# Batch 0 of a linear-attention kernel: the first q rows by sixteen small activations, dense work begun on one head pair, the other q rows in pairs

## Chip, cores and metric

The kernel runs on one core of a Trainium2 chip. The metric is the time of one launch in microseconds of device time, lower is better. Five engines work beside one another, each on its own list of instructions in order: TensorE (PE), VectorE (DVE), ScalarE (ACT), GpSimd (POOL) and SyncE (SP). Transfers are asked for by SP ("SPq") and by POOL, and are carried out by 16 DMA engines.

## The reference

q, k and v are float32 of shape (8, 8, 576, 64): batch, heads, rows, head size. The two weights are 512 x 2048 and 2048 x 512.

```
q_s = softmax of q over the head size
k_s = softmax of k over the 576 rows
kv  = einsum('bhsd,bhse->bhde', k_s, v)
att = einsum('bhsd,bhde->bhse', q_s, kv)
x   = att, heads joined: 4608 x 512
h   = x @ w_in
out = maximum(0.01 * h, h) @ w_out
```

## The kernel before

One partition holds 9 successive rows of two heads at a time (R = 9 "q rows" per partition, 64 partitions per head; `HL` = 4 head groups), so a q or k tile of one batch is 128 x 4 x 9 x 64. The output is made in nine tiles of 512 tokens (t = 0 to 8). A tile has a first dense layer (`layer1`, 16 column blocks j of w_in; then `leaky` on ACT) and a second (`layer2`, 16 blocks j of w_out). Tile 0 needs 512 of the 576 tokens of batch 0, so nothing dense can run before batch 0's attention; the attention of each later batch is woven into the dense work of earlier tiles. The scheduling is manual: the order of the Python calls is the order on each engine. The function `at(t, u, ...)` hangs calls on place u of tile t: in tile 0, places 0 to 31 follow block j of the first layer (first 256 tokens, then the other 256), and 32 to 47 follow the blocks of the second layer.

Batch 0 goes so (lines of the kernel before):

- L90 to L97: SP asks for q rows 0 to 3 (`RA`), k in two halves, v in two halves, then q rows 4 to 8 (`RB`).
- `q_max`, `q_sub` (POOL), `q_exp` (ACT), `q_sum`, `q_norm` (L221 to L253) are q's softmax: greatest value of each row, subtraction, exponential, sum with reciprocal, product.
- `k_tree` (L151 to L160): four DVE operations that take the maximum over the 9 rows of a partition, for one half (two head groups). `k_max_pe` (L301) turns it with a transpose on PE, `k_all_dve` and `k_all_pe` (L311, L315) take the maximum over partitions and spread it, `k_sub_ps` (L325) subtracts it, `k_exp` (L200) makes the exponential.
- `v_cast` (L207): v to bfloat16. `kv_pair` (L332): k'v for one pair of head groups. `kd_pair` (L346): divides by k's sum and keeps the blocks on the diagonal. `q_transpose`, `q_keep` (L360, L376): q turned on PE and copied out of PSUM. `attend` (L385): q times kv, copied to xT, the input of the dense layer.
- `wake(n)` (L295): n matmuls on zeros whose results are not used.
- POOL's list after setting constants: `q_sub` of rows RA; a copy of one element into `gate` (L483), which waits until k's second half has landed; `load_w_in(0)` (four transfers, the first half of w_in's columns, L133); the two `v_cast`; `load_w_in(1)`; `q_sub` of RB; a second `gate` copy (L525), which waits for k of batch 1; four transfers of w_out (L140). What stands below it on POOL's list follows later: `k_sub` of batch 1 and so on.
- SP's list goes on with `hold_sync(0)` (L521), a small transfer that reads the end of w_in's columns and so waits for the first transfer of `load_w_in(1)`; then k, q, v of batch 1; then `hold_sync(1)`, which waits for a transfer of w_out; then batch 2.
- L532 to L548, hooks of tile 0: rows RB are turned at place 11 and attended at 13; batch 1's k maxima, subtractions and q maxima are called at place 15; batch 1's k'v (`kv(1)`, L261) is at place 38.

PSUM has a ring of six banks (`psB_pool`) for all of these results.

Of the kernel before, what the change touches and what calls it, by code (L numbers as in the profile page):

```python
# [8 lines left out]
FP32 = mybir.dt.float32  # L9
# [11 lines left out]
R = 9  # L21
HL = 4
# [3 lines left out]
def kernel(  # L26
# [112 lines left out]
    def load_w_out(fq):
        nc.gpsimd.dma_start(  # L140
            out=w_out_sb[:, 4 * fq : 4 * fq + 4, :], in_=w_out_r[:, 4 * fq : 4 * fq + 4, :]
        )
# [8 lines left out]
    def k_tree(b, hs):  # L151
        n = hs.stop - hs.start
        ks = st[b]["k"][:, hs]
        t4 = mx_pool.tile([P, HL, 4, D], FP32, name="t4")[:, 0:n]
        nc.vector.tensor_tensor(out=t4, in0=ks[:, :, 0:4], in1=ks[:, :, 4:8], op=ALU.max)  # L155
        t2 = t4[:, :, 0:2]
        nc.vector.tensor_tensor(out=t2, in0=t2, in1=t4[:, :, 2:4], op=ALU.max)  # L157
        t1 = t4[:, :, 0]
        nc.vector.tensor_tensor(out=t1, in0=t1, in1=t4[:, :, 1], op=ALU.max)  # L159
        nc.vector.tensor_tensor(out=st[b]["kmax"][:, hs], in0=t1, in1=ks[:, :, 8], op=ALU.max)  # L160
# [60 lines left out]
    def q_max(b, rs):  # L221
        n = rs.stop - rs.start
        st[b]["qmax", rs.start] = m = small_pool.tile([P, HL, n], FP32, name="qmax")
        nc.vector.tensor_reduce(out=m, in_=st[b]["q"][:, :, rs], axis=AX.X, op=ALU.max)  # L224

    def q_sub(eng, b, rs):
        n = rs.stop - rs.start
        qs = st[b]["q"][:, :, rs]
        eng.tensor_tensor(  # L229
            out=qs,  # L230
            in0=qs,
            in1=st[b]["qmax", rs.start].unsqueeze(3).to_broadcast([P, HL, n, D]),
            op=ALU.subtract,
        )
# [60 lines left out]
    def wake(n):  # L295
        for i in range(n):
            nc.tensor.matmul(  # L297
                wake_ps, lhsT=zero[:, 0:P], rhs=zero, start=(i == 0), stop=(i == n - 1)
            )

    def k_max_pe(b, i):  # L301
        ps = psB_pool.tile([P, 2, L], FP32, name="kT", tag=BANK_TAG)
        nc.tensor.matmul(
            ps.rearrange("c h l -> c (h l)"),
            lhsT=st[b]["kmax"][:, 2 * i : 2 * i + 2].rearrange("p h d -> p (h d)"),
            rhs=identf,
            is_transpose=True,
        )
# [37 lines left out]
    def kd_pair(b, gg):  # L346
        for hh in range(2):
            pkv = st[b]["pkv", gg][hh]
            krec = small_pool.tile([P, 1], FP32, name="krec1")
            nc.vector.reciprocal(out=krec, in_=pkv[:, 128:129])  # L350
            nc.vector.scalar_tensor_tensor(
                out=kd2[b % 2][:, 2 * hh + gg],
                in0=pkv[:, 0:P],
                scalar=krec,
                in1=block,
                op0=ALU.mult,
                op1=ALU.mult,
            )

    def q_transpose(b, r0, n):  # L360
# [57 lines left out]
        else:  # L418
            eng.tensor_copy(out=o, in_=ps)

    def layer1(j, ph, c0, n):
        for i, cb in enumerate((0, 2, 1, 3)):
            nc.tensor.matmul(  # L423
                ph,
                lhsT=w_in_sb[:, cb, j * P : (j + 1) * P],
                rhs=xT[:, cb, c0 : c0 + n],
                start=(i == 0),
                stop=(i == NB - 1),
            )

    def leaky(o, ph):
# [91 lines left out]
    st[1]["q"] = load(q, 1, "q_raw", [(ALLH, ALLR)])  # L523
    st[1]["v"] = load(v, 1, "v_raw", [(ALLH, ALLR)])
    nc.gpsimd.tensor_copy(out=gate[:, 0:1], in_=st[1]["k"][:, 0, 0, 0:1])  # L525
# [12 lines left out]
    at(0, 15, lambda: q_max(1, RA), lambda: q_sub(nc.gpsimd, 1, RA))  # L538
# [125 lines left out]
```

## Time and profile before

Three runs took 302.57, 301.48 and 302.45 us, median 302.45. The profile is of one execution more.

| what | value |
|---|---|
| profiled execution: its time, its span | 300.17 us, 298.4 us |
| PE busy | 283.0 us, 95% of the span |
| DVE, ACT, POOL busy | 151.6, 143.0, 89.0 us |
| chain that ended last, by engine | PE 85%, DVE 8%, ACT 2%, DMA 2%, POOL 1%, issue 1% |
| first dense matmul after which PE has no long wait | 24.31 us after the start |
| PE busy in 24:26 of the span | 1.69 us of 2.00 |
| PE busy in 32:36 of the span | 4.00 us of 4.00 |
| q rows 0 to 3: maximum (DVE), subtraction (POOL), exponential (ACT) | 1.22, 1.90, 1.06 us |
| bytes moved by transfers in the first 60 us | 15.47 MB, mean 258 GB/s |

A line of the timeline or of the chain begins with the start and the duration in us, measured from the span's start. In a timeline line the engine, the line of the kernel, the operation, output and input, shapes and the count follow, and in brackets the idle time of the engine before it with what ended it. A line of the table by stage has the stretch, its length, the busy time of PE, of PE's weight loads, of DVE, ACT and POOL (with the number of instructions), TensorE's granted clock as a share of the full one, the DMA engines' busy share and the bytes moved per second.

### The profile page before, as it was taken

Reading aid. Unit: us, or ns where it says so; the run is one execution under the profiler, and the core shown is the slowest. Engines: PE = TensorE matmul, PEld = TensorE weight load, DVE = VectorE, ACT = ScalarE, POOL = GpSimd, SP = SyncE. Lnnn points to the kernel's source line nnn. Section 1 sums busy time; section 2 is a strip of 40 time slices with the busy share of each in tenths; the row PEclk is TensorE's granted clock in tenths of the full one; section 3 lists DMA queues with packets and bytes.
Section 4 is the critical chain, followed back from the end, with each engine's and each line's share of the span. In section 5 each row is a group of like instructions: output and inputs, shape, how many; then the busy total and the mean of one; then the engine's idle time right before and its main releaser. Section 6 shows DMA issues by size and latency. Waiting matters only on the chain.

```text
span 298.4 us, 4180 instructions
## 1 busy us (share of the span) xinstructions
PE 283.0 (95%) x1638; PEld 138.5 (46%) x1638; DVE 151.6 (51%) x234; ACT 143.0 (48%) x233; POOL 89.0 (30%) x60
## 2 busy tenths in 40 slices
PE   6388999999899999999999999999999999999993
PEld 2137855444444454454445444544454444444441
DVE  3996869691975299079548354835440200110020
ACT  1146675669037903971485428542854066016400
POOL 6926081008008604900940193009400000000000
PEclk9579999999999999999999999999999999999999
DMA  7999999396086844765379137923141310130033
GB/s 260 307 227 384 236 201 375 75 296 250 16 170 196 316 79 106 251 262 115 74 253 335 38 70 250 313 63 70 37 79 35 73 35 0 41 85 16 0 73 70
DMA packets 36371, 45.75 MB, mean 153 GB/s; under 512 B 15872, under 2 KB 18944, under 8 KB 36352
## 3 DMA queue, kind: packets, MB, share of 16 engines
q1 hardware_dynamic: 33088, 41.30, 46.7%
q0 software_dynamic: 3264, 4.20, 8.0%
q8 instruction: 13, 0.21, 0.3%
q14 instruction: 6, 0.05, 0.1%
HBM read 36.70 MB, written 9.44 MB: 155 GB/s over the span
## 4 chain that ended last, share of the span: by engine, by line
PE 85%; DVE 8%; ACT 2%; DMA 2%; POOL 1%; issue 1%; SPq 0%; POOLq 0%
PE pout L444 40%; PE ph L423 39%; PE pkv L268 3%; PE po L411 2%; DMA k_raw<-in_k_dram 2%; DVE t L155 1%; POOL k_raw L193 1%; DVE t L157 1%; DVE k_raw L328 1%; ACT vb L211 1%; DVE kmax L160 1%; DVE t L159 1%; ACT xT L397 1%; DVE xT L399 1%; PE psum_qt L364 1%
## 5 line engine op out<-in xcount | busy, mean ns | idle before, releaser
L444 PE MATMUL pout<-w_out_sb,gj 128*128 128x512 bf16 x576 | 130.9, 380 | 0.7 <-DVE out_sb L438 0.7
L423 PE MATMUL ph<-xT,w_in_sb 128*128 128x512 bf16 (+1 forms) x640 | 127.4, 358 | 0.7 <-DVE xT L399 0.6
L432 ACT ACTIVATE gj<-ph 128x512 bf16<-128x512 f32 x144 | 82.6, 603 | 58.8 <-PE ph L423 58.1
L423 PEld LDWEIGHTS <-w_in_sb 128*128 128x128 bf16 x640 | 62.2, 98 | 62.8 <-issue 1.9
L444 PEld LDWEIGHTS <-gj 128*128 128x128 bf16 x576 | 55.8, 98 | 63.0 <-issue 1.0
L438 DVE COPY out_sb<-pout 128x512 f32<-128x512 f32 x36 | 24.5, 687 | 88.9 <-PE pout L444 83.2
L193 POOL TENSOR_TENSOR k_raw<-k_raw,kall 128x2304 f32<-128x2304 f32 (+1 forms) x6 | 29.1, 4844 | 92.1 <-DVE kall L185 76.0
L229 POOL TENSOR_TENSOR q_raw<-q_raw,qmax 128x2304 f32<-128x2304 f32 (+2 forms) x10 | 32.7, 3273 | 29.5 <-DVE qmax L224 24.0
L246 DVE TENSOR_REDUCE qsum<-qe 128x36 f32<-128x2304 bf16 (+2 forms) x10 | 20.7, 2072 | 38.7 <-ACT qe L237 38.6
L417 ACT CAST xT<-po 128x320 bf16<-128x320 f32 (+1 forms) x48 | 16.8, 402 | 39.4 <-PE po L411 39.4
L201 ACT ACTIVATE ke<-k_raw 128x2304 bf16<-128x2304 f32 (+1 forms) x10 | 17.4, 1737 | 24.6 <-POOL k_raw L193 15.6
L224 DVE TENSOR_REDUCE qmax<-q_raw 128x36 f32<-128x2304 f32 (+2 forms) x10 | 20.5, 2061 | 4.8 <-DMA q_raw<-in_q_dram 4.8
L253 DVE TENSOR_TENSOR qe<-qe,qrec 128x2304 bf16<-128x2304 bf16 (+2 forms) x10 | 20.8, 2078 | 0.3
L237 ACT ACTIVATE qe<-q_raw 128x2304 bf16<-128x2304 f32 (+2 forms) x10 | 17.4, 1744 | 6.3 <-POOL q_raw L229 6.3
L213 POOL CAST vb<-v_raw 128x1152 bf16<-128x1152 f32 x14 | 16.0, 1170 | 0.0
L155 DVE TENSOR_TENSOR t<-k_raw 128x1024 f32<-128x1024 f32 (+1 forms) x10 | 11.6, 1165 | 0.5 <-DMA k_raw<-in_k_dram 0.3
L297 PE MATMUL pout<-zero 128*128 128x512 bf16 x24 | 10.0, 595 | 1.3 <-POOL zero L100 1.3
L411 PE MATMUL po<-qX,kd 128*128 128x320 bf16 (+1 forms) x48 | 9.8, 286 | 0.0
L268 PEld LDWEIGHTS <-ke 64*128 64x128 bf16 x252 | 7.2, 93 | 3.3 <-ACT gj L432 1.7
L268 PE MATMUL pkv<-vb,ke 64*128 64x129 bf16 x252 | 8.6, 217 | 0.2 <-ACT vb L211 0.2
L286 DVE TENSOR_TENSOR kd<-pkv,krec 64x128 bf16<-64x128 f32 x28 | 8.1, 288 | 0.7
L411 PEld LDWEIGHTS <-kd 128*128 128x128 bf16 x48 | 4.6, 98 | 5.9 <-DMA qX<-qe 0.5
(50 smaller groups left out, 90.9 us busy)
## 6 DMA issues: line engine op xcount, KB each, us to landing
out_dram<-out_sb SPq DMA_DIRECT2D x72, 128.0 KB, 2.4
q_raw<-in_q_dram SPq DMA_DIRECT2D x7, 1152.0 KB, 8.2
v_raw<-in_v_dram SPq DMA_DIRECT2D x7, 1152.0 KB, 11.4
k_raw<-in_k_dram SPq DMA_DIRECT2D x6, 1152.0 KB, 5.8
k_raw<-in_k_dram SPq DMA_DIRECT2D x4, 576.0 KB, 5.2
w_in_sb<-in_moe_w_in_dram POOLq DMA_DIRECT2D x8, 256.0 KB, 6.0
w_out_sb<-in_moe_w_out_dram POOLq DMA_DIRECT2D x4, 512.0 KB, 13.4
v_raw<-in_v_dram SPq DMA_DIRECT2D x2, 576.0 KB, 7.5
```

Source lines behind the costliest of these rows:

```text
L193: eng.tensor_tensor(out=ks, in0=ks, in1=st[b]["kall"][:, hs].unsqueeze(2).to_broadcast([P, n, R, D]), op=ALU.subtract,)
L201: nc.scalar.activation(out=st[b]["ke"][:, :, hs].rearrange("p r h d -> p h r d"), in_=st[b]["k"][:, hs], func=AF.Exp,)
L224: nc.vector.tensor_reduce(out=m, in_=st[b]["q"][:, :, rs], axis=AX.X, op=ALU.max)
L229: eng.tensor_tensor(out=qs, in0=qs, in1=st[b]["qmax", rs.start].unsqueeze(3).to_broadcast([P, HL, n, D]), op=ALU.subtract,)
L246: nc.vector.reduce_sum(out=qsum, in_=st[b]["qe"][:, rs], axis=AX.X)
L253: nc.vector.tensor_tensor(out=qes, in0=qes, in1=st[b]["qrec", rs.start].unsqueeze(3).to_broadcast([P, n, HL, D]), op=ALU.mult,)
L268: nc.tensor.matmul(pkv[hh][:, gg, 0:129], lhsT=st[b]["ke"][rows, r, 2 * gg : 2 * gg + 2].rearrange("p h d -> p (h d)"), rhs=vb2[b % 2][row ...
L411: nc.tensor.matmul(ps.rearrange("p (r l) -> p r l", l=L), lhsT=kd2[b % 2][:, g], rhs=qX[:, gg, hh, rs])
L423: nc.tensor.matmul(ph, lhsT=w_in_sb[:, cb, j * P : (j + 1) * P], rhs=xT[:, cb, c0 : c0 + n], start=(i == 0), stop=(i == NB - 1),)
L432: nc.scalar.activation(out=o, in_=ph, func=AF.Prelu, alpha=LEAKY_SLOPE)
L438: nc.vector.tensor_copy(out=out_sb, in_=pout)
L444: nc.tensor.matmul(pout, lhsT=g_sb[j // 2][:, j % 2, tsub * P : (tsub + 1) * P], rhs=w_out_sb[:, j, :], start=(j == 0), stop=(j == NF - 1),)
```

## The change

The q rows of batch 0 are cut anew: RA stays rows 0 to 3; RB is cut into R1 (rows 4, 5), R2 (rows 6, 7) and R3 (row 8). In the order of the lists:

- SP asks for rows RA in two transfers of 256 KB (heads 0 and 1, then 2 and 3) where there was one of 512 KB.
- Rows RA: `q_max`, the subtraction on POOL, one exponential of 128 x 1024 and one sum on DVE are replaced by `q_first`: two DVE maxima that write the negated value, and sixteen ACT exponentials of 128 x 64, each with its row's negated maximum as a bias and an added sum output. The reciprocal of the sums stays on DVE (`q_first_rec`).
- On DVE, `k_all_dve(0, 0)` stands after the first operation of the second half's tree; the first half's `k_sub_ps` is cut in two by head group, with an exponential after each. `q_max` of rows RB no longer stands ahead of `kd`.
- `q_keep` of the second half of RA goes from ACT to DVE. One of the four diagonal blocks is made on ACT by two scalings of 64 x 64.
- `wake` goes from 12, 4 and 8 matmuls to 16, 1, 1, 2 and 1.
- The first 256 tokens: six blocks j begin with the contributions of heads' pairs 0 and 2, in three banks, before `attend(0, [1, 3])`, and are finished after it.
- POOL's list is now: gate; `load_w_in(0)`; two `v_cast`; `load_w_in(1)`; `q_sub` of R1; the second gate, which waits for k of batch 1; five transfers of w_out (blocks 0-1, 2-3, 4-7, 8-11, 12-15) where there were four; `q_sub` of R2; `q_sub` of R3; `k_sub` of batch 1 and so on.
- ACT's list in tile 0 is: three `leaky`; exponential of R1; one `leaky`; exponential of R2; three `leaky`; xT of pairs 0 and 2; four `leaky`; exponential of R3; and so on.
- DVE's list after `kd` is: `q_max` R1, `q_max` R2; sum, reciprocal and product of R1, the same of R2; `q_keep` of R1 and of R2; xT of pairs 1 and 3; `q_max` R3; then the k tree of batch 1.
- PE's list: R1 is turned at place 9, R2 at place 12 (between the matmuls of j = 12 and j = 13), both are attended at place 14; R3, which tile 1 needs first, is turned at place 37 and attended at 40. Batch 1's hooks stay where they were.

```diff
+    R1, R2, R3 = slice(4, 6), slice(6, 8), slice(8, R)
-    st[0]["q"] = load(q, 0, "q_raw", [(ALLH, RA)])
+    st[0]["q"] = load(q, 0, "q_raw", [(slice(0, 2), RA), (slice(2, 4), RA)])
...
+    def q_first(b, rs):
+        n = rs.stop - rs.start
+        nmax = small_pool.tile([P, HL, n], FP32, name="nmax")
+        qsum = small_pool.tile([P, n, HL], FP32, name="qsum")
+        for hs in (slice(0, 2), slice(2, 4)):
+            nc.vector.tensor_reduce(
+                out=nmax[:, hs], in_=st[b]["q"][:, hs, rs], axis=AX.X, op=ALU.max, negate=True
+            )
+            for h in range(hs.start, hs.stop):
+                for r in range(n):
+                    nc.scalar.activation(
+                        out=st[b]["qe"][:, rs.start + r, h],
+                        in_=st[b]["q"][:, h, rs.start + r],
+                        func=AF.Exp,
+                        bias=nmax[:, h, r : r + 1],
+                        accum_out=qsum[:, r, h : h + 1],
+                    )
+        st[b]["qsum"] = qsum
...
+        if eng is nc.scalar:
+            for p0 in range(0, P, D):
+                ps = slice(p0, p0 + D)
+                nc.scalar.mul(out=o[ps, ps], in_=pkv[ps, ps], mul=krec[ps])
...
-    wake(12)
+    HA, HB = slice(0, 1), slice(1, 2)
+    wake(16)
     k_begin(0)
     q_begin(0)
-    q_max(0, RA)
-    q_sub(nc.gpsimd, 0, RA)
+    q_first(0, RA)
     nc.gpsimd.tensor_copy(out=gate[:, 0:1], in_=st[0]["k"][:, HL - 1, R - 1, D - 1 : D])
     load_w_in(0)
     k_tree(0, H0)
     k_max_pe(0, 0)
-    wake(4)
-    k_tree(0, H1)
-    k_max_pe(0, 1)
+    wake(1)
+    k_tree(0, H1, slice(0, 1))
     k_all_dve(0, 0)
     k_all_pe(0, 0)
+    k_tree(0, H1, slice(1, 4))
+    k_max_pe(0, 1)
+    wake(1)
+    k_sub_ps(0, 0, HA)
+    k_exp(0, slice(0, 1))
     k_all_dve(0, 1)
     k_all_pe(0, 1)
-    wake(8)
-    q_exp(0, RA)
-    q_sum(0, RA)
-    k_sub_ps(0, 0)
-    k_exp(0, H0)
+    wake(2)
+    k_sub_ps(0, 0, HB)
+    k_exp(0, slice(1, 2))
     k_sub_ps(0, 1)
     k_exp(0, H1)
     v_cast(nc.gpsimd, 0, 0)
     v_cast(nc.gpsimd, 0, 1)
     load_w_in(1)
+    q_first_rec(0, RA)
     q_norm(0, RA)
-    q_max(0, RB)
-    q_sub(nc.gpsimd, 0, RB)
     kv_pair(0, 0)
+    wake(1)
     q_transpose(0, 0, 4)
     kv_pair(0, 1)
+    for hh in range(2):
+        kd_rec(0, 0, hh)
+        kd_one(nc.vector, 0, 0, hh)
     q_keep(nc.scalar, 0, 0, 4, slice(0, 4, 2))
-    kd_pair(0, 0)
-    q_keep(nc.scalar, 0, 0, 4, slice(1, 4, 2))
+    q_keep(nc.vector, 0, 0, 4, slice(1, 4, 2))
+    kd_rec(0, 1, 1)
+    kd_one(nc.scalar, 0, 1, 1)
+    kd_rec(0, 1, 0)
+    kd_one(nc.vector, 0, 1, 0)
     attend(0, [0, 2], 0, 256, nc.scalar)
-    kd_pair(0, 1)
-    attend(0, [1, 3], 0, 256, nc.vector)
-    q_exp(0, RB)
-    q_sum(0, RB)
-    q_norm(0, RB)
+    q_max(0, R1)
+    q_sub(nc.gpsimd, 0, R1)
...
-    for fq in range(4):
-        load_w_out(fq)
+    for j0, j1 in ((0, 2), (2, 4), (4, 8), (8, 12), (12, 16)):
+        load_w_out(slice(j0, j1))
...
-    at(0, 11, lambda: q_transpose(0, 4, 3), lambda: q_transpose(0, 7, 2))
-    at(0, 11, lambda: q_keep(nc.vector, 0, 4, 3), lambda: q_keep(nc.vector, 0, 7, 2))
-    for g in range(NB):
-        at(0, 13, lambda g=g: attend(0, [g], 256, 320, (nc.scalar, nc.vector)[g % 2]))
+    at(0, 5, lambda: q_max(0, R2), lambda: q_sub(nc.gpsimd, 0, R2))
+    at(0, 5, lambda: q_exp(0, R1), lambda: q_sum(0, R1), lambda: q_norm(0, R1))
+    at(0, 7, lambda: q_exp(0, R2), lambda: q_sum(0, R2), lambda: q_norm(0, R2))
+    at(0, 9, lambda: q_transpose(0, 4, 2), lambda: q_keep(nc.vector, 0, 4, 2))
+    at(0, 12, lambda: q_transpose(0, 6, 2), lambda: q_keep(nc.vector, 0, 6, 2))
+    at(0, 14, lambda: attend(0, [0, 2], 256, 256, nc.scalar))
+    at(0, 14, lambda: attend(0, [1, 3], 256, 256, nc.vector))
+    at(0, 15, lambda: q_max(0, R3), lambda: q_sub(nc.gpsimd, 0, R3))
+    at(0, 21, lambda: q_exp(0, R3))
+    at(0, 32, lambda: q_sum(0, R3), lambda: q_norm(0, R3))
+    at(0, 37, lambda: q_transpose(0, 8, 1), lambda: q_keep(nc.scalar, 0, 8, 1))
+    at(0, 40, lambda: attend(0, [0, 1, 2, 3], 512, 64, nc.scalar))
...
+    begun = []
+    for j in range(0, 6, 2):
+        ph = psB_pool.tile([P, 2, 256], FP32, name="ph", tag=BANK_TAG)
+        for i in range(2):
+            layer1(j + i, ph[:, i], 0, 256, slice(0, 2), i == 0)
+        begun.append(ph)
+    attend(0, [1, 3], 0, 256, nc.scalar)
     for half in range(2):
         for j in range(0, NF, 2):
-            ph = psB_pool.tile([P, 2, 256], FP32, name="ph", tag=BANK_TAG)
+            part = slice(2, 4) if begun else slice(0, 4)
+            ph = begun.pop(0) if begun else psB_pool.tile([P, 2, 256], FP32, name="ph", tag=BANK_TAG)
             for i in range(2):
-                layer1(j + i, ph[:, i], 256 * half, 256)
+                layer1(j + i, ph[:, i], 256 * half, 256, part, i == 0, i == 1)
```

More of the change, by code (lines that the diff above doesn't have):

```diff
@@ L137, with load_w_out @@
     w_out_r = moe_w_out.rearrange("(fb f) o -> f fb o", f=P)
[L139 to L142, printed above, removed]
+    def load_w_out(js):
+        nc.gpsimd.dma_start(out=w_out_sb[:, js, :], in_=w_out_r[:, js, :])
     def k_begin(b):
@@ L149, in k_begin, with k_tree @@
         st[b]["kall"] = mx_pool.tile([P, HL, D], FP32, name="kall")
-    def k_tree(b, hs):
+    def k_tree(b, hs, steps=slice(0, 4)):
         n = hs.stop - hs.start
         ks = st[b]["k"][:, hs]
[L154 to L160, printed above, removed]
+        if steps.start == 0:
+            st[b]["t4"] = mx_pool.tile([P, HL, 4, D], FP32, name="t4")[:, 0:n]
+        t4 = st[b]["t4"]
+        t2, t1 = t4[:, :, 0:2], t4[:, :, 0]
+        for o, i0, i1 in (
+            (t4, ks[:, :, 0:4], ks[:, :, 4:8]),
+            (t2, t2, t4[:, :, 2:4]),
+            (t1, t1, t4[:, :, 1]),
+            (st[b]["kmax"][:, hs], t1, ks[:, :, 8]),
+        )[steps]:
+            nc.vector.tensor_tensor(out=o, in0=i0, in1=i1, op=ALU.max)
     def k_allmax(b):
@@ L224, in q_max, with q_first_rec @@
         nc.vector.tensor_reduce(out=m, in_=st[b]["q"][:, :, rs], axis=AX.X, op=ALU.max)
+    def q_first(b, rs):
[16 more added lines that the diff above has]
+        st[b]["qsum"] = qsum
+    def q_first_rec(b, rs):
+        n = rs.stop - rs.start
+        st[b]["qrec", rs.start] = qrec = small_pool.tile([P, n, HL], FP32, name="qrec")
+        nc.vector.reciprocal(out=qrec, in_=st[b]["qsum"])
     def q_sub(eng, b, rs):
@@ L323, in k_all_pe, with k_sub_ps @@
         st[b]["kallp", i] = ps
-    def k_sub_ps(b, i):
-        ks = st[b]["k"][:, 2 * i : 2 * i + 2]
-        a = st[b]["kallp", i].rearrange("p (h d) -> p h d", d=D)
+    def k_sub_ps(b, i, hs=slice(0, 2)):
+        ks = st[b]["k"][:, 2 * i + hs.start : 2 * i + hs.stop]
+        a = st[b]["kallp", i].rearrange("p (h d) -> p h d", d=D)[:, hs]
+        n = hs.stop - hs.start
         nc.vector.tensor_tensor(
-            out=ks, in0=ks, in1=a.unsqueeze(2).to_broadcast([P, 2, R, D]), op=ALU.subtract
+            out=ks, in0=ks, in1=a.unsqueeze(2).to_broadcast([P, n, R, D]), op=ALU.subtract
         )
@@ L344, in kv_pair, with kd_rec, kd_one @@
         st[b]["pkv", gg] = pkv
[L346 to L350, printed above, removed]
-            nc.vector.scalar_tensor_tensor(
[L352 to L357, printed above, removed]
+    def kd_rec(b, gg, hh):
+        st[b]["krec", gg, hh] = krec = small_pool.tile([P, 1], FP32, name="krec1")
+        nc.vector.reciprocal(out=krec, in_=st[b]["pkv", gg][hh][:, 128:129])
+    def kd_one(eng, b, gg, hh):
+        pkv, krec = st[b]["pkv", gg][hh], st[b]["krec", gg, hh]
+        o = kd2[b % 2][:, 2 * hh + gg]
+        if eng is nc.scalar:
+            for p0 in range(0, P, D):
+                ps = slice(p0, p0 + D)
+                nc.scalar.mul(out=o[ps, ps], in_=pkv[ps, ps], mul=krec[ps])
+        else:
+            nc.vector.scalar_tensor_tensor(
+                out=o, in0=pkv[:, 0:P], scalar=krec, in1=block, op0=ALU.mult, op1=ALU.mult
             )
@@ L419, in attend_x, with layer1 @@
             eng.tensor_copy(out=o, in_=ps)
-    def layer1(j, ph, c0, n):
-        for i, cb in enumerate((0, 2, 1, 3)):
+    def layer1(j, ph, c0, n, part=slice(0, 4), first=True, last=True):
+        for i, cb in list(enumerate((0, 2, 1, 3)))[part]:
             nc.tensor.matmul(
@@ L426, in layer1 @@
                 rhs=xT[:, cb, c0 : c0 + n],
-                start=(i == 0),
-                stop=(i == NB - 1),
+                start=(i == 0 and first),
+                stop=(i == NB - 1 and last),
             )
```

## The prediction

> **What bounds the kernel now.** I read the chain that ended last first: it is PE without a gap worth naming from 24.31 us on, save one short wait at 46.2, and a DVE chain ahead of it. So a change to batch 0 counts in two places: when the dense work gets going, and whether it then runs on without waiting. From the chain, the place where RB is turned and the end of batch 1's chain:
>
> ```profile
> 24.31 5.18 PE ph L423 x46
> 29.50 0.56 PE psum_qt L364 x10
> 30.05 0.87 PE ph L423 x8
> ...
> 32.19 0.61 DVE t L155
> ...
> 45.13 1.06 ACT vb L211
> 46.18 0.04 issue
> 46.23 0.69 PE pkv L268 x18
> ```
>
> PE waits a little at 46.23 for ACT's cast, which ends a chain that began on DVE at 32.10 (tree of batch 1). PE alone would have been there at about 45.4, so batch 1's chain, 14.1 us from the tree's start, is ahead of PE by 0.9 us: whoever delays the tree delays the end.
>
> The timeline of DVE shows what the change is after. The same four operations take 1.81 us at 32.10 and 5.0 us at 6.26, where POOL works on SBUF beside them:
>
> ```profile
> 6.26 2.25 DVE L155 TENSOR_TENSOR t<-k_raw 128x512 f32<-128x512 f32 x1 [0.29 <-DMA k_raw<-in_k_dram]
> ...
> 9.32 1.27 DVE L160 TENSOR_TENSOR kmax<-t,k_raw 128x128 f32<-128x128 f32 x1
> ...
> 11.35 1.25 DVE L157 TENSOR_TENSOR t<-t 128x256 f32<-128x256 f32 x1
> ...
> 32.10 0.68 DVE L155 TENSOR_TENSOR t<-k_raw 128x512 f32<-128x512 f32 x1
> 32.82 0.42 DVE L157 TENSOR_TENSOR t<-t 128x256 f32<-128x256 f32 x1
> ```
>
> The timeline of POOL shows the row that decides, to my mind:
>
> ```profile
> 21.43 2.33 POOL L229 TENSOR_TENSOR q_raw<-q_raw,qmax 128x1280 f32<-128x1280 f32 x1 [5.51 <-DVE krec L350]
> 24.03 0.19 POOL L525 COPY gate<-k_raw 128x1 f32<-128x1 f32 x1 [0.27 <-DMA k_raw<-in_k_dram]
> 24.49 3.04 POOL L140 DMA_DIRECT2D w_out_sb<-in_moe_w_out_dram  x4 [0.28 <-issue]
> ```
>
> The second gate waits for batch 1's k, which lands at 24.0, and the w_out issues hold POOL until 27.53. Before the change all of RB's subtraction is over by then; R2's and R3's now stand behind it. What sets 24.0 is in the table by stage: SP asks for that k from 19.29, but bytes move at some 209 GB/s (w_in) until about 21.5 and only then at 410.
>
> ```profile
> 20.00:21.00 1.00, 0.99 (x24) 0.90 (x26) 1.00 (x1) 0.35 (x2) 0.00 (x0) 1.00 1.12 209
> 21.00:22.00 1.00, 0.38 (x11) 0.16 (x5) 0.93 (x5) 0.74 (x2) 0.57 (x1) 1.00 1.10 267
> 22.00:23.00 1.00, 0.64 (x3) 0.19 (x2) 0.93 (x5) 0.35 (x1) 1.00 (x1) 1.00 1.04 410
> ```
>
> The DMA engines' share (second number from the end) is above 1 from 4 us to here, so this k comes when everything asked for before it is through. The change asks for the same bytes in the same order: 24.0 stays, within 0.5 us.
>
> **The front, part by part.** k's first half lands at 6.2, as before; the two half maxima of q (0.67 us each, from 1.22 for 1024 elements) are over before it. The extra issue of q puts k back by 0 to 0.45 us (one SP issue); I take 0, since the engines are filled with q meanwhile. DVE then: tree without POOL's subtraction 1.81, first operation of the next 0.72, kr 0.3, rest of the tree 1.1, one collision with the w_in issues as at 9.32 (0.98; 0 to 2): 11.2. k_sub half, kr, half, whole: 0.67 + 0.3 + 0.67 + 1.3, to 14.1. Reciprocal and q_norm 0.17 + 1.2, to 15.5; two kd 0.92. PE: transposes 0.62 and kv_pair 0.7, to 16.8; q_keep on DVE, two small ACT scalings (0.2 each, as the 0.206 of one element), xT 0.58: 18.2. Twelve matmuls at 0.113 are 1.35, attend 0.3, xT 0.6: 20.5, with twelve matmuls done where before there were two at 24.31. The front gains 24.31 - 20.5 + 10 x 0.113 = 4.9 us. Removed from DVE's path are 1.14 (sum), 1.4 (qmax of RB) and some 3 of collisions.
>
> The sixteen small exponentials have no row. From below: 0.206 us each (the one-element row), 3.3 together; from above two such rows, one of them for the sum, and 0.06 for 64 elements at the 0.9 ns that lie between the ACT rows of 512 and 1024: 0.47, 7.6 together, for the one of 1.06 removed. They start at about 4.3 and are wanted by 13.9, so either end is covered. The cover goes at 0.6 us each on that path.
>
> The Trainium skill, "ScalarE: Activation LUTs", section "What ACT_TABLE_LOAD costs", speaks against this edit: an activation with a pointer bias costs a fixed 280 ns or so beside 0.833 ns per element, and neighbours overlap by about 93 ns. That would be an estimated 0.24 us each, 3.8 us together; no row here shows it, and the end would be the same.
>
> **The wait that replaces it.** PE goes on from 20.5: twelve second halves 1.35, sixteen matmuls 1.8, R1 turned when its q_norm is done (three leaky at 0.6 after 20.95, exponential 0.62, then 1.6 on DVE: 24.9; PE waits 1.25), 0.28, then twelve matmuls up to j = 12 at 26.55. There it needs R2 normalized. R2, from rows: gate at 24.03, issue from 24.49; three transfers of 0.774 and two of half size at 0.39 to 0.774, I take 0.65 (near the 0.617 of a w_in issue): 3.6, to 28.1 (27.6 to 28.4). POOL's subtraction of 512 elements 1.04 (line through 1.896 for 1024 and 2.327 for 1280): 29.15. Exponential 0.62 (same way): 29.8; ACT stands still for it, its leaky queued behind. Sum, reciprocal, product 0.67 + 0.20 + 0.68 and gaps: 31.4. Transposes 0.28: 31.7. So PE stands some 4.9 us, and the front's gain is spent here whatever it was.
>
> After that: j = 13 and 14 0.9, four attends 0.5, xT 0.7, qmax of R3 0.4, to 34.25, where batch 1's tree begins; before it was 32.10: +2.15. POOL's subtraction of R3 (256 elements, 0.6) falls on the tree's first operation, as it did at 6.26: 0 to 0.6, I take 0.3. Batch 1's chain keeps its 14.1 us behind that, its w_out and v transfers being no later: +2.45 (1.9 to 3.1) at 46.23. PE itself would be later by 31.7 + 0.1 for R3's transposes, against 30.34 for j = 13 before: 1.5, less than the chain, so it waits 1 us there. Behind 46.2 PE was full, so the shift stays to the end. R3's own steps (DVE 1 us, ACT 0.8, from the rows by size) lie where DVE had waited 3.2 us at 45.16, and ahead of ACT's q_keep at 49.87; there is nothing to charge.
>
> **The clock.** The granted clock fell at 8.57, 2.6 us after the last wake's end at 5.96, and came back at 18.8, after 4.7 us of nearly unbroken matmuls:
>
> ```profile
> 8.50:8.75 0.25, 0.00 (x0) 0.00 (x0) 0.22 (x2) 0.25 (x1) 0.25 (x2) 0.65 1.03 387
> ...
> 18.75:19.00 0.25, 0.25 (x2) 0.00 (x0) 0.25 (x2) 0.16 (x2) 0.00 (x0) 0.87 1.17 221
> ```
>
> A stand of 4.9 us is longer than 2.6, so the work behind it may begin at half clock. The blocks and attends before xT would then cost 1.4 us more (0.9 + 0.5 again); PE's own 4.7 us at half rate lose 2.35, to 3.85 late, as much as the chain. So 0 to 1.4, and I take 0.7: a few idle microseconds may fall across two of whatever stretches the clock is judged by. A slow clock already in the front (fewer wakes) costs at most the front's 5 us and is covered by the same stand.
>
> The Trainium skill, "TensorE: Matmul & The Clock Gate", Part 1, has the clock fall after an idle window of about 3.4 us that runs free of the kernel, and return after as much sustained work. By that the loss is an estimated 1.7 us of PE, which the chain's lead would partly hide; the sum would stay at its warm or its cold end by where the window falls.
>
> **Sum.** +2.45 + 0.7 = +3.15: 303.3 against the profiled 300.17, and 305.6 against the median of the runs, 302.45, which lies 2.3 above that execution. This is the time I give; the case's own range is +1.9 to +4.5, 304.3 to 307.0.
>
> **Rivals.** (1) Faster: k of batch 1 lands early enough for POOL to get to R2 in time. Then R2 is normalized at 26.3 and PE does not stand; the tree begins at about 29.5 and batch 1's chain ends 2.6 us earlier: 299.8. The tree starts 6.15 after R2's subtraction does, so the break-even is a start at 25.7, a landing at 21.6. For it speaks that 18.62, when SP is let through, is early; against it that w_in fills the engines until 21.5. Chance 0.17. (2) No change: landing near 21.6, or part of the shift made up where ACT and PE interleave at 50 to 58 (the chain there has waits of under 0.1 us, which speaks against it): 302.5. Chance 0.12. (3) The small activations or the front pass the 4.9 us of cover: at 1.1 us each the sums end at 22 where 14 was wanted, 8 late, 3.1 beyond the cover: 302.45 + 3.15 + 3.1, about 309. No row is near that price. Chance 0.04.
>
> **How the numbers follow.** The forecast has 0.67. Half a per cent, 1.5 us, is about what a measurement of this kernel can tell from no change. Slower by more: forecast and rival 3, 0.71; within it 0.12; faster 0.17. For 8 in 10 I leave out rival 1's lower half and rival 3: 300.3 to 307.8.
>
> **What would show it.** Right: R2's subtraction on POOL starts at about 28, directly behind the w_out issues; PE idles 3 to 5 us ahead of R2's transposes near 31.5; batch 1's tree starts at 34 to 35; the first half's tree takes under 2 us at 6.3. Wrong: the second gate before 22, R2's transposes before 28, or matmuls behind the stand that run unbroken with batch 1's tree before 32.

## The result, and the profile after

The changed kernel takes 309.46 us (median of four runs, 309.00 to 310.09) against 302.42 us for the kernel before beside it (four runs, 301.48 to 302.57): a ratio of 1.0241, 95% interval 1.0211 to 1.0270. So it is slower, as forecast, but by 7.0 us where 3.15 were forecast, and 309.46 lies outside the stated range of 300.3 to 307.8. The profiled execution took 310.09 us with a span of 308.2; its mean granted clock was 0.97, before 0.983.

The timeline of the changed kernel, with start and duration in us, shows the place that the prediction turned on:

```profile
10.74 0.30 POOL L514 COPY gate<-k_raw 128x1 f32<-128x1 f32 x1 [6.73 <-DMA k_raw<-in_k_dram]
...
29.69 0.19 POOL L561 COPY gate<-k_raw 128x1 f32<-128x1 f32 x1 [5.26 <-DMA k_raw<-in_k_dram]
...
30.16 3.72 POOL L141 DMA_DIRECT2D w_out_sb<-in_moe_w_out_dram  x5 [0.28 <-issue]
...
33.85 1.09 POOL L257 TENSOR_TENSOR q_raw<-q_raw,qmax 128x512 f32<-128x512 f32 x1
34.98 0.63 ACT L265 ACTIVATE qe<-q_raw 128x512 bf16<-128x512 f32 x1 [4.17 <-POOL q_raw L257]
...
37.44 0.58 PE L395 MATMUL psum_qt<-ident,qe 128*128 128x128 bf16 x4 [3.59 <-DVE qe L281]
...
41.55 0.68 DVE L163 TENSOR_TENSOR t<-k_raw 128x512 f32<-128x512 f32 x1
```

From the second gate downward it is the forecast's story: gate, w_out issues, R2's subtraction behind them, exponential, R2's transposes with PE standing ahead of them, then batch 1's tree. But the gate opens at 29.69, not at 24.03. The first gate is late as well (10.74, before 7.90, where it came straight behind POOL's subtraction of RA). In the changed kernel both wait for a transfer of k. Batch 1's tree is 9.45 us later than before (32.10), its last k'v 9.73 us later (55.96 for 46.23), and the span is 9.8 us longer: nothing is won or lost behind that.

The chain that ended last has transfers in it that were not there before. Its early part (start, duration, engine, what):

```profile
2.26 8.42 DMA k_raw<-in_k_dram
...
15.68 7.47 DMA w_in_sb<-in_moe_w_in_dram
23.83 5.74 DMA k_raw<-in_k_dram
30.16 3.72 POOL w_out_sb L141 x5
```

In the table by stage the last number is GB/s and the one ahead of it the DMA engines' busy share. Two stretches of the kernel before:

```profile
4.00:6.00 2.00, 1.96 (x7) 0.52 (x4) 1.22 (x1) 0.00 (x0) 0.01 (x1) 1.00 1.04 409
...
18.00:20.00 2.00, 1.69 (x21) 0.66 (x19) 2.00 (x3) 1.91 (x2) 0.00 (x0) 0.80 1.12 209
```

The same stretches of the changed kernel:

```profile
4.00:6.00 2.00, 2.00 (x7) 0.60 (x5) 0.98 (x2) 1.57 (x9) 0.01 (x1) 1.00 0.83 206
...
18.00:20.00 2.00, 2.00 (x21) 0.99 (x19) 1.97 (x3) 1.13 (x2) 0.08 (x1) 0.50 1.09 158
36.00:40.00 4.00, 2.56 (x15) 1.93 (x16) 1.98 (x5) 1.18 (x3) 0.00 (x0) 0.66 1.23 218
```

Half the bytes move in 4:6, while k of batch 0 is under way, and a quarter fewer in 18:20, while w_in is; in 18:20 the engines are as busy as before. The trace holds each packet's duration. k's packets (2304 bytes) that start between 3.5 and 6 us, and w_in's (2048 bytes) between 16 and 22 us, in ns:

```
kernel        k packets  median  95%   longest    w_in packets  median  95%  longest
before            361       93     93     101          578         173    173     173
changed           197       93    412    1704          475         173    360     766
```

Most packets are as quick as before, and a few take up to 18 times as long. The last line of the table above (36:40) shows the clock (third number from the end) at 0.66 behind PE's stand.

### The profile page after: what moved, and what is told of

It reads as the page before. It is cut to its first block, busy times and chain, and to the rows that moved or that the text cites. A ratio compares the mean times of both kernels' runs of the same rounds, so it can differ in the third digit from the quotient of the medians.

```text
span 308.2 us, 4204 instructions
## 1 busy us (share of the span) xinstructions
PE 284.0 (92%) x1613; PEld 139.9 (45%) x1639; DVE 150.8 (49%) x241; ACT 148.6 (48%) x270; POOL 88.1 (29%) x62
## 4 chain that ended last, share of the span: by engine, by line
PE 79%; DMA 7%; POOL 4%; DVE 3%; ACT 2%; issue 1%; SPq 1%; POOLq 0%; ACTq 0%
PE pout L475 38%; PE ph L454 36%; DMA k_raw<-in_k_dram 5%; DMA w_in_sb<-in_moe_w_in_dram 2%; PE pkv L296 2%; PE po L442 2%; POOL k_raw L196 1%; POOL w_out_sb L141 1%; DVE t L163 1%; POOL w_in_sb L134 1%; ACT vb L214 1%; POOL vb L216 1%; ACT xT L428 1%; ACT qe L265 1%; PE psum_qt L395 1%
## 5 line engine op out<-in xcount | busy, mean ns | idle before, releaser
L454 PE MATMUL ph<-xT,w_in_sb 128*128 128x512 bf16 (+1 forms) x627 | 129.2, 362 | 3.2 <-ACT xT L428 2.2
L274 DVE TENSOR_REDUCE qsum<-qe 128x36 f32<-128x2304 bf16 (+4 forms) x11 | 19.8, 1800 | 45.8 <-ACT qe L265 45.8
L257 POOL TENSOR_TENSOR q_raw<-q_raw,qmax 128x2304 f32<-128x2304 f32 (+4 forms) x11 | 31.8, 2894 | 34.0 <-DVE qmax L227 34.0
L204 ACT ACTIVATE ke<-k_raw 128x2304 bf16<-128x2304 f32 (+2 forms) x11 | 17.6, 1597 | 24.6 <-POOL k_raw L196 15.6
L281 DVE TENSOR_TENSOR qe<-qe,qrec 128x2304 bf16<-128x2304 bf16 (+4 forms) x12 | 22.2, 1851 | 0.4
L227 DVE TENSOR_REDUCE qmax<-q_raw 128x36 f32<-128x2304 f32 (+4 forms) x11 | 19.5, 1788 | 0.0
L265 ACT ACTIVATE qe<-q_raw 128x2304 bf16<-128x2304 f32 (+4 forms) x11 | 16.8, 1525 | 4.3 <-POOL q_raw L257 4.2
L163 DVE TENSOR_TENSOR t<-k_raw 128x1024 f32<-128x1024 f32 (+1 forms) x10 | 10.1, 1010 | 4.4 <-DMA k_raw<-in_k_dram 4.2
L163 DVE TENSOR_TENSOR t<-t 128x256 f32<-128x256 f32 (+2 forms) x20 | 10.8, 540 | 0.6
L395 PE MATMUL psum_qt<-ident,qe 128*128 128x128 bf16 x36 | 3.5, 228 | 5.8 <-DVE qe L281 5.8
```

Source lines behind the costliest of these rows:

```text
L163: nc.vector.tensor_tensor(out=o, in0=i0, in1=i1, op=ALU.max)
L257: eng.tensor_tensor(out=qs, in0=qs, in1=st[b]["qmax", rs.start].unsqueeze(3).to_broadcast([P, HL, n, D]), op=ALU.subtract,)
L265: nc.scalar.activation(out=st[b]["qe"][:, rs].rearrange("p r h d -> p h r d"), in_=st[b]["q"][:, :, rs], func=AF.Exp,)
L274: nc.vector.reduce_sum(out=qsum, in_=st[b]["qe"][:, rs], axis=AX.X)
L281: nc.vector.tensor_tensor(out=qes, in0=qes, in1=st[b]["qrec", rs.start].unsqueeze(3).to_broadcast([P, n, HL, D]), op=ALU.mult,)
L454: nc.tensor.matmul(ph, lhsT=w_in_sb[:, cb, j * P : (j + 1) * P], rhs=xT[:, cb, c0 : c0 + n], start=(i == 0 and first), stop=(i == NB - 1 a ...
```

## The experiments

The time of the kernel before on the chips of these runs was 300.65 (runs 1 to 4), 301.68 (5 to 8), 301.34 (9 to 11) and 300.76 us (12). "k lands" is the start of the first operation of batch 0's tree, which waits for k.

| kernel | median us | ratio to before, 95% interval | k lands | second gate | tree of batch 1 |
|---|---|---|---|---|---|
| before | | | 6.26 | 24.03 | 32.10 |
| changed | 309.46 | 1.0241 (1.0211 to 1.0270) | 9.19 | 29.69 | 41.55 |
| 1 changed, once more | 308.13 (one run) | | 8.69 | 27.89 | 39.75 |
| 2 R2 ahead of the gate | 303.04 | 1.0066 (1.0034 to 1.0099) | 8.00 | 27.38 | 31.59 |
| 3 one load of q | 303.99 | 1.0106 (1.0086 to 1.0125) | 6.62 | 24.60 | 35.01 |
| 4 old softmax of RA | 308.68 | 1.0239 (1.0192 to 1.0287) | 8.93 | 30.18 | 42.01 |
| 5 before, with the cut | 301.24 | 0.9989 (0.9965 to 1.0013) | 8.39 | 28.65 | 31.02 |
| 6 both of 2 and 3 | 302.18 | 1.0022 (0.9998 to 1.0047) | 6.44 | 24.68 | 32.58 |
| 7 6 with the old softmax of RA | 303.49 | 1.0080 (1.0051 to 1.0109) | 6.50 | 25.68 | 34.61 |
| 8 changed, cut by rows | 308.73 | 1.0225 (1.0172 to 1.0278) | 8.46 | 28.53 | 40.40 |
| 9 6 with v casts on ACT | 299.46 | 0.9932 (0.9910 to 0.9954) | 6.52 | 25.14 | 31.32 |
| 10 9 with earlier exponentials | 298.81 | 0.9911 (0.9882 to 0.9941) | 6.37 | 25.38 | 30.50 |
| 11 before, v casts on ACT | 298.66 | 0.9922 (0.9892 to 0.9952) | 6.37 | 24.82 | 31.40 |
| 12 10 with more dummy matmuls | 298.39 | 0.9912 (0.9890 to 0.9935) | 6.45 | 24.90 | 28.99 |

**1. The changed kernel once more.** Nothing is edited; the question is whether the slow transfers belong to the kernel or to one execution.

> The changed kernel once more, to see whether its slow transfers belong to it. In its first profile batch 0's k landed at 9.2 us (6.2 before the change) and batch 1's k at 29.7 (24.0). If the kernel makes the transfers slow, both come again within 1 us and the time is 309 to 310. If they were chance, they land at about 6.2 and 24 and the time is the 305 to 306 of the prediction's sum.

k lands at 8.69, the gate opens at 27.89, and k's packets in 3.5 to 6 us again include long ones (longest 1442 ns). The delay belongs to the kernel; its size varies by some 2 us (the gate is 1.8 us earlier than in the first profile, and the one time is 308.13, where 309 to 310 was expected).

**2. R2 ahead of the second gate.** The forecast's mechanism is taken away; the cut load stays.

```diff
     q_sub(nc.gpsimd, 0, R1)
+    q_max(0, R2)
+    q_sub(nc.gpsimd, 0, R2)
...
-    at(0, 5, lambda: q_max(0, R2), lambda: q_sub(nc.gpsimd, 0, R2))
```

> R2's maximum and subtraction called before the second gate, all else as changed. Theory of the wait (R2's subtraction stands behind the gate and the w_out issues on POOL): PE no longer stands ahead of R2's transposes, batch 1's tree starts at about 36.4 instead of 41.55, time about 304.4. If only the late landing counts and not what is queued behind it, the time stays at 309.

```profile
20.06 2.04 POOL L257 TENSOR_TENSOR q_raw<-q_raw,qmax 128x512 f32<-128x512 f32 x2 [3.04 <-DVE qmax L227]
...
27.38 0.19 POOL L563 COPY gate<-k_raw 128x1 f32<-128x1 f32 x1 [5.27 <-DMA k_raw<-in_k_dram]
...
28.93 0.38 PE L395 MATMUL psum_qt<-ident,qe 128*128 128x128 bf16 x4
...
31.59 0.68 DVE L163 TENSOR_TENSOR t<-k_raw 128x512 f32<-128x512 f32 x1
```

The timeline shows both subtractions done at 22.1, R2's transposes without a wait, and batch 1's tree half a microsecond earlier than in the kernel before, although the gate still opens 3.4 us late. The ratio falls from 1.0241 to 1.0066. What hangs on the gate, then, is R2, as the prediction had it. The tree is far earlier than the 36.4 that I had expected, and the time 1.4 us below the expected 304.4. But this profile is of the fastest of ten executions (300.70 to 304.96 us), and in it DVE's last tree operation of batch 0 took 0.29 us at 12.31, where the changed kernel's took 2.37 (more in run 9). So not all of the 9.96 us by which the tree is earlier need come from the edit, and the 0.7% that remain can't be read from this profile.

**3. One load of q.** The order behind the gate stays; only the cut is undone.

```diff
-    st[0]["q"] = load(q, 0, "q_raw", [(slice(0, 2), RA), (slice(2, 4), RA)])
+    st[0]["q"] = load(q, 0, "q_raw", [(ALLH, RA)])
```

> The first q rows asked for in one transfer again, all else as changed. Theory that the cut transfer slows the others: batch 0's k lands at about 6.2, batch 1's at about 24, time 305 to 306. Rival, that the small activations or something else slows them: 9.2, 29.7 and 309 as before.

```profile
24.60 0.19 POOL L561 COPY gate<-k_raw 128x1 f32<-128x1 f32 x1 [2.50 <-DMA k_raw<-in_k_dram]
25.06 3.72 POOL L141 DMA_DIRECT2D w_out_sb<-in_moe_w_out_dram  x5 [0.27 <-issue]
...
28.75 1.10 POOL L257 TENSOR_TENSOR q_raw<-q_raw,qmax 128x512 f32<-128x512 f32 x1
...
32.34 0.39 PE L395 MATMUL psum_qt<-ident,qe 128*128 128x128 bf16 x4 [2.05 <-DVE qe L281]
...
35.01 0.68 DVE L163 TENSOR_TENSOR t<-k_raw 128x512 f32<-128x512 f32 x1
```

This is, in its order, the timeline that the prediction described: gate within 0.6 us of 24.0, tree 10.41 us behind it (10.22 in the prediction's sum), tree to last k'v 14.40 (14.1). The time is 3.3 us above the kernel before, 3.15 in the forecast. The transfers are quick again (the longest of w_in's packets in 16 to 22 us takes 173 ns). So what the changed kernel loses beyond the forecast goes with the cut. (I had expected 305 to 306 us, reckoned from a kernel before at 302.45; on this chip it took 300.65.) That the loss agrees so closely is in part luck: PE stood 2.05 us ahead of R2's transposes, not 4.9, and the clock stayed at 1.00 behind it, so the 0.7 us charged for the clock didn't occur; a gate 0.57 us late and 0.19 us more from the gate to the tree took their place.

**4. The old softmax of RA, with the cut.** This asks whether the ACT work of the small exponentials, or their reading of q, disturbs the transfers.

```diff
-    q_first(0, RA)
+    q_max(0, RA)
+    q_sub(nc.gpsimd, 0, RA)
...
+    q_exp(0, RA)
+    q_sum(0, RA)
-    q_first_rec(0, RA)
```

> The first q rows by the old steps (maximum, subtraction on POOL, one exponential, sum on DVE), all else as changed, the two transfers of q too. Theory that the sixteen small activations with sums slow the transfers: batch 0's k lands at 6.2 to 6.7 and batch 1's at about 24, time 305 to 306.5 (POOL's subtraction meets the tree again, which the stand ahead of R2 hides). Rival, that the cut transfer or something else does: 9.2, 29.7, 309 to 310.

The transfers are as slow without the small exponentials: k lands at 8.93, the gate opens at 30.18, the time is that of the changed kernel.

**5. The kernel before with only the cut.**

```diff
-    st[0]["q"] = load(q, 0, "q_raw", [(ALLH, RA)])
+    st[0]["q"] = load(q, 0, "q_raw", [(slice(0, 2), RA), (slice(2, 4), RA)])
```

> The kernel before with nothing but the first q load cut in two by heads. Theory that the cut alone slows the transfers: batch 0's k lands at 8 to 9.2 us instead of 6.2, batch 1's at 27 to 30 instead of 24, and the time is 3 to 5 us over the kernel before. Rival, that the cut only hurts beside the other edits (more wakes, no work of POOL's at the start): 6.2 to 6.7, 24 and no change.

```profile
20.21 2.33 POOL L229 TENSOR_TENSOR q_raw<-q_raw,qmax 128x1280 f32<-128x1280 f32 x1 [2.94 <-DVE krec L350]
...
28.65 0.19 POOL L525 COPY gate<-k_raw 128x1 f32<-128x1 f32 x1 [6.11 <-DMA k_raw<-in_k_dram]
...
31.02 0.68 DVE L155 TENSOR_TENSOR t<-k_raw 128x512 f32<-128x512 f32 x1
```

I had expected a loss of several microseconds, and there is none (0.9989). The transfers are slow here too: k at 8.39, gate 4.6 us late, k packets up to 1542 ns. But in this kernel nothing of batch 0 stands behind the second gate: rows RB are subtracted at 20.21, ahead of it. And k's lateness at the front is paid back, since POOL's subtraction of RA is over (7.63) when k's tree begins, and the tree's first half runs in 1.8 us instead of 4.3. The same cut costs this kernel nothing and the changed one 3.7 us: that loses 7.0 us with the cut and 3.3 without it (run 3). The two kernels differ in more than the place of the subtraction; run 6 compares the two orders in one kernel.

**6. Both repairs.** The edits of 2 and 3 together.

> The change with both repairs: R2's subtraction before the second gate, and q in one load. If the two account for the whole loss and their costs add: the time is that of the kernel before within 1 us (batch 1's tree near 32.1; the front lost 2 to 3 us to the casts on POOL against the sum in the prediction). If the front's gain of 4.9 is there as predicted, 2 to 3 us faster than before. If something else is slower still, 302 or more against 300.65.

1.0022 (0.9998 to 1.0047): no measurable loss is left, and no gain. Cut and order together account for the 2.4%, and the change as a whole wins nothing yet. The tree of batch 1 starts at 32.58, 0.5 us later than before. Runs 2, 3 and 6 with the changed kernel make up all four cases: with R2 behind the gate the cut costs 1.35% (1.0241 against 1.0106), with R2 ahead of it 0.44% (1.0066 against 1.0022, whose intervals overlap).

**7. Run 6 with the old softmax of RA.** The edit of run 4 on run 6, with RA's one exponential called earlier, ahead of the first `k_sub_ps`.

> As the run with both repairs, but the first q rows by the old steps (maximum on DVE, subtraction on POOL, one exponential, sum on DVE). If the sixteen small activations gain what the prediction's front says (1.2 of sum and reciprocal on DVE, and POOL's subtraction off the tree, 1.6): 2 to 3 us slower than with both repairs. If the front is hidden behind R1's and R2's normalization or w_in's landing: the same within 0.5 us.

The tree's first operation takes 2.25 us again under POOL's subtraction, batch 1's tree is 2.0 us later than in run 6, and the time 1.3 us longer. That is what the small exponentials, in place of the old steps, are worth where nothing covers it, less than the 2 to 3 us that I had expected.

**8. The cut made by rows.** Heads stay together; rows 0, 1 and rows 2, 3 are loaded apart.

```diff
-    st[0]["q"] = load(q, 0, "q_raw", [(slice(0, 2), RA), (slice(2, 4), RA)])
+    st[0]["q"] = load(q, 0, "q_raw", [(ALLH, slice(0, 2)), (ALLH, slice(2, 4))])
```

> The changed kernel with the first q load cut by rows (0, 1 and 2, 3; all heads in each) instead of by heads. If any second transfer at the front upsets the others: batch 0's k lands at 8 to 9.5, time 307 to 310. If it is the cut by heads: k lands at 6.5 to 7 (the packets are half as large, some 0.3 us more), batch 1's at 24 to 25, time 304 to 306.

The same as the changed kernel: k at 8.46, gate at 28.53, k packets up to 1694 ns. It isn't this cut by heads, but two loads where there was one. What in the second load does it is not taken apart: in all six profiles with the cut SP also asks for k half a microsecond later (at 1.75, before at 1.25), and no run delays k without the cut.

**9. The v casts on ACT.** In run 6 DVE's last tree operation of batch 0 took 2.39 us instead of 0.29, beside POOL's two v casts; the changed kernel has the same at 13.56:

```profile
11.84 1.69 DVE L163 TENSOR_TENSOR t<-t 128x256 f32<-128x256 f32 x2
13.51 2.27 POOL L216 CAST vb<-v_raw 128x1152 bf16<-128x1152 f32 x2
13.56 2.37 DVE L163 TENSOR_TENSOR kmax<-t,k_raw 128x128 f32<-128x128 f32 x1
```

So the casts go to ACT, which stands idle there.

```diff
+    v_cast(nc.scalar, 0, 0)
     wake(1)
     k_sub_ps(0, 0, HA)
...
     k_exp(0, slice(1, 2))
+    v_cast(nc.scalar, 0, 1)
...
-    v_cast(nc.gpsimd, 0, 0)
-    v_cast(nc.gpsimd, 0, 1)
```

> The changed kernel with one first q load and with R2's maximum and subtraction ahead of the second gate (302.18 us, kernel before 302.4 to 302.5 in all runs so far), and with batch 0's two v casts moved from POOL to ACT, where ACT has waits of 2.81 and 0.86 us. Theory (the front's gain was eaten by VectorE's last tree operation, 10.79 for 2.39 us, held through the two casts): that operation takes 0.29 us, batch 0's chain is about 1.7 us earlier at its k'v, the first dense matmul too, batch 1's tree starts near 30.9 instead of 32.58, and the time is 300 to 301 us, 0.992 to 0.996 of the kernel before. Rival (the dense work's start was not what bounded it, since R1's exponential waits behind three leaky and w_in's and k's transfers don't move): 301.7 to 302.5, tree of batch 1 after 32.

The timeline of this run at the same operations, with POOL's w_in issues beside them:

```profile
8.31 4.93 POOL L134 DMA_DIRECT2D w_in_sb<-in_moe_w_in_dram  x8
...
9.17 0.74 DVE L163 TENSOR_TENSOR t<-t 128x256 f32<-128x256 f32 x2
9.94 0.29 DVE L163 TENSOR_TENSOR kmax<-t,k_raw 128x128 f32<-128x128 f32 x1
```

The three operations take 1.03 us instead of 4.06, and 0.9932 of the kernel before is reached. The tree of batch 1 starts at 31.32, a little behind the 30.9 expected. (The kernel before had been at 300.65 and 301.68 us in the runs up to here, not at 302.4 to 302.5.)

**10. Earlier exponentials of R1 and R2.** In run 6 DVE waits 5.01 us for R1's exponential, which stands behind three `leaky` on ACT.

```diff
-    at(0, 5, lambda: q_exp(0, R1), lambda: q_sum(0, R1), lambda: q_norm(0, R1))
-    at(0, 7, lambda: q_exp(0, R2), lambda: q_sum(0, R2), lambda: q_norm(0, R2))
+    at(0, 1, lambda: q_exp(0, R1), lambda: q_sum(0, R1), lambda: q_norm(0, R1))
+    at(0, 3, lambda: q_exp(0, R2), lambda: q_sum(0, R2), lambda: q_norm(0, R2))
```

> The same, with the exponentials, sums and products of R1 and R2 hooked behind blocks 1 and 3 instead of 5 and 7, so that R1's exponential stands behind one leaky and R2's behind two. Theory: VectorE's wait of 5.01 us for R1's exponential shrinks, PE's wait of 1.47 us at R1's transposes goes, batch 1's tree starts near 29.7, and the time is 298.5 to 300 us, 0.986 to 0.993 of the kernel before, the fastest of all. Rival: ACT then delays leaky and with it the banks of PE, what is won at the tree is lost there: the same as the kernel without the earlier hooks within 0.5 us.

PE's wait at R1's transposes goes from 1.47 to 0.49 us, the tree starts 0.8 us earlier, 0.9911. The intervals of runs 9 and 10 overlap, so this step alone isn't shown to gain.

**11. The kernel before with the casts on ACT.**

```diff
     q_exp(0, RA)
+    v_cast(nc.scalar, 0, 0)
+    v_cast(nc.scalar, 0, 1)
...
-    v_cast(nc.gpsimd, 0, 0)
-    v_cast(nc.gpsimd, 0, 1)
```

> The kernel before with the two v casts of batch 0 on ACT behind the first exponential, nothing else changed. VectorE's two tree operations of 1.25 and 1.11 us (11.35 to 13.7) fall to 0.42 and 0.29, batch 0's chain is 1.6 us earlier. If such collisions are worth their time at the end: 0.993 to 0.997 of the kernel before, and the comparison for the two kernels above. If VectorE's queue ahead of batch 1's tree is held by something else (the subtraction of rows RB behind k's transfer): within 0.2 per cent.

```profile
8.60 4.93 POOL L133 DMA_DIRECT2D w_in_sb<-in_moe_w_in_dram  x8
...
9.43 0.29 DVE L160 TENSOR_TENSOR kmax<-t,k_raw 128x128 f32<-128x128 f32 x1
...
10.49 0.42 DVE L157 TENSOR_TENSOR t<-t 128x256 f32<-128x256 f32 x1
...
10.95 0.29 DVE L159 TENSOR_TENSOR t<-t 128x128 f32<-128x128 f32 x1
```

0.9922 (0.9892 to 0.9952), from moving two instructions, slightly more than the 0.993 to 0.997 expected. The operations shown took 1.27, 1.25 and 1.11 us before. Runs 10 and 11 can't be told apart: with the casts away, nothing more of the change is shown to be worth its place.

**12. More dummy matmuls.** In run 10 the clock was at 0.50 from 13 to 22 us and the first twelve dense matmuls took 2.72 us.

```diff
-    wake(16)
+    wake(20)
...
-    wake(2)
+    wake(7)
```

> The kernel with casts on ACT and early exponentials (298.81 us, 0.9911 of the kernel before), with 20 instead of 16 dummy matmuls at the start and 7 instead of 2 ahead of the first k'v, where PE waits 1.28 us. In that kernel the granted clock was 0.79 at 12 to 13 us and 0.50 from 13 to 22, and the twelve first dense matmuls took 2.72 us instead of 1.47. Theory (the clock falls because PE stands too much from 7 to 13 us, and that costs batch 0's end): clock 1.00 from 12 to 22, twelve matmuls in 1.5 us, k'v in 0.7 instead of 1.16, batch 1's tree 1.5 to 2 us earlier than 30.5, and 296.5 to 298 us, 0.983 to 0.988 of the kernel before. Rival (the added matmuls stand in the way of batch 0's transposes, or the wait moves to w_in's second half, whose bytes end near 22): tree within 0.5 us of 30.5, time within 0.7 us of 298.8.

Half of this came true. The clock still falls at 11.7, but is back at 1.00 from 15.1; the twelve matmuls take 1.47 us, and batch 1's tree starts 1.5 us earlier. The span is only 0.7 us shorter than in run 10, and the ratio is the same, 0.9912; the time, 298.39, is above the 296.5 to 298 expected. The chain that ended last now runs through two transposing transfers of later batches (from 156 to 163 us and from 187 to 193), where run 10's runs through one (from 187), so a part of the gain may be waited away there. What sets those transfers' time I didn't follow up.

## Why the prediction was wrong in size, and right in mechanism

**The step that failed.** "The change asks for the same bytes in the same order: 24.0 stays, within 0.5 us." The bytes and their order are the same, and the gate opened at 29.69 (5.66 late). The same error stands at the front: "k's first half lands at 6.2, as before", with 0 to 0.45 us for one more issue; it was 2.9 us. I had looked at bytes and at the engines' busy share, and had no term for the duration of a packet. The way from there, in the timeline of the kernel before:

```profile
7.90 0.65 POOL L483 COPY gate<-k_raw 128x1 f32<-128x1 f32 x1
...
13.54 2.38 POOL L133 DMA_DIRECT2D w_in_sb<-in_moe_w_in_dram  x4
...
18.62 0.62 SPq L475 DMA_DIRECT2D held<-w_in_sb  x1
...
19.29 1.08 SPq L79 DMA_DIRECT2D k_raw<-in_k_dram  x2
```

In the changed kernel the first gate is 2.84 us late, so the first transfer of `load_w_in(1)` is issued at 15.68 (2.14 late); it lands 7.47 us behind its issue (5.1 before, 13.54 to 18.62); SP's hold lets k of batch 1 go at 23.83 instead of 19.29; and that k takes 5.74 us, where it took 4.7. Run 3 puts the gate back at 24.60 by undoing the cut alone, run 6 at 24.68 with the order undone as well, and runs 4, 5 and 8 keep it late with other work, in another kernel and with another cut.

**The terms.** In the profiled executions the change is 9.92 us, against 3.15. The gate is 5.66 of the difference. The half clock behind the stand is another 0.75: the gate to tree stretch took 11.86 us, and 10.41 in run 3, whose clock stayed at 1.00, so the term is 1.45, its upper end (1.4), where I took 0.7. Of the remaining 0.36, 0.19 lies between gate and tree (10.41 in run 3, 10.22 in the sum) and the rest behind the last k'v. In the medians the miss is 3.9, because the execution of the kernel before that was profiled was among its fastest, while the changed kernel's profiled one was its slowest.

**What held.** The w_out issues took 3.72 us (3.6), R2's subtraction 1.09 (1.04), its exponential 0.63 (0.62), sum, reciprocal and product 0.69, 0.20 and 0.69; the tree to k'v 14.4 (14.1). The sixteen small exponentials were 0.333 us apiece from start to start, 5.3 together (3.3 to 7.6 in the bounds), and were covered: the estimate from the Trainium skill, "ScalarE: Activation LUTs", section "What ACT_TABLE_LOAD costs", was 0.24 apiece. The trace has 0.24 from an activation's start to that of the 0.19 us instruction for its sum, and 0.09 from there to the next activation: the sum is the difference.

**The front.** I gave it 4.9 us. In run 3, with quick transfers, twelve dense matmuls were done and PE went on from 23.67, where it had two done at 24.31: 0.64 + 10 x 0.113 = 1.8. The mis-sized term is the collisions: one of 0.98 us in the sum, two of 0.93 and 2.10 in run 3 as in run 6, which is 2.05 of the 3.1 that are missing; the rest I haven't assigned. As the prediction said, what the front gains is spent at R2 in any case, so this miss costs nothing in the result; with the casts away (run 9) the kernel is faster than the one before. The prediction put that collision down to the w_in issues; runs 9 and 11 show that it goes with the casts.

**Two readings of the kernel before.** The first half's tree at 6.26 took 4.3 us (to 10.59), not 5.0. And batch 1's chain was not 0.9 us ahead of PE at 46.23: PE was at work on the other half of k'v from 45.37 to 46.06 and then waited 0.17. Neither carries the sum, in which the chain came later by more than PE did.

**Rivals.** None of the three happened. (1) needed the landing earlier than 21.6, and it came later. (2) "no change" is what the kernel before shows under the same cut (run 5), but not this one. (3) gave about 309, which is the measured time, by a mechanism that the trace excludes: exponentials of 0.333 us where it took them at 1.1. A rival on the transfers themselves, later k by some microseconds, was missing; with 10.2 us of chain behind the gate its price could have been read from the same rows, one for one.

## What to carry to other kernels

That the bytes are the same does not make one more issue at the head of a busy queue free: compare the landing times of what follows, in the trace, before trusting them. Put nothing of an earlier stage behind a gate that waits for a later stage's data; then a late transfer costs little: nothing measurable in run 5, 0.44% between runs 2 and 6, 1.35% in the changed kernel. And look for small operations with far too long a duration beside GpSimd work: moving two casts to an idle engine brought 0.8% here, and nothing else is shown to bring more.

## What the runs showed of the hardware

**Two loads for one slow what comes later.** In all six profiles with the cut (the changed kernel and runs 1, 2, 4, 5 and 8) k lands between 8.0 and 9.2 us and the longest of its packets in 3.5 to 6 us takes 992 to 1704 ns; in all eight without it k lands between 6.3 and 6.6 and the longest takes 93 to 387 ns. The disturbance still shows at 16 to 22 us, long after the cut load has landed: 73 to 133 of w_in's 460 to 513 packets take over 180 ns there, without the cut 0 to 35 of 558 to 601. Why is open: the packets tell that a few are slow, not what they wait for.

**A cast on GpSimd holds a VectorE operation longer than the rows show.** One 0.29 us operation took 2.37 us through two casts one after the other, and the operations ahead of it took 1.69 us for 0.75 while the row of POOL showed w_in issues. My prediction put that down to the issues. Runs 9 and 11 have the same issues at the same operations and no casts, and the operations run at full speed: the delay needs the casts queued behind the issues. How they hold an operation ahead of their own row in the profile is not shown. The Trainium skill, "SBUF — State Buffer", section "SBUF: two separate sides", has a VectorE operation with two SBUF inputs and a GpSimd operation that reads SBUF lock each other out for one whole instruction, and the loser waits; the runs agree on who collides, and differ in that the wait went through two instructions.

**The clock falls behind stands of 3 us, and behind a shorter one too.** PE stands of 3.02, 3.16, 3.34 and 3.59 us (runs 4, 8, 1, the changed kernel) were followed by four transposes in 0.56 to 0.59 us; after one of 2.05 us (run 3) they took 0.39. But the changed kernel lost the clock once more, ahead of its first dense matmuls and behind a stand of 1.48 us (22.16 to 23.65):

```profile
20.25:23.66 3.41, 1.63 (x29) 1.26 (x30) 2.90 (x11) 1.79 (x4) 0.27 (x1) 1.00 1.07 185
23.66:27.07 3.41, 3.13 (x14) 2.07 (x14) 0.24 (x1) 0.24 (x1) 0.77 (x1) 0.50 0.99 239
```

The first twelve took 2.72 us there and 1.47 in run 3, which the stand ahead of R2 then hid. PE was busy for 1.63 of the 3.41 us before this fall; in run 3 it was busy for 1.61 us of 28.68 to 32.09, and the clock stayed at 1.00. So neither the length of one stand nor PE's busy share decides it alone, and what does is not shown. The Trainium skill, "TensorE: Matmul & The Clock Gate", Part 1, names an idle window of about 3.4 us; of the five stands here that lost the clock, four are shorter than that.
